# Linear attention and an MLP on one core: key sums and attention products as two matmuls of 64 stationary columns each

## The chip, the cores and the metric

The kernel runs on one core of a Trainium2 chip. The metric is the device time of one execution in microseconds (us), given as the median of several runs; lower is better.

## What is computed

Eight batches of 576 tokens, eight heads of 64 dimensions, and 128 random features. Queries and keys become positive features, keys and values are summed over a batch's tokens, and each query row is multiplied with these sums. The result, 4608 rows of 512, goes through a layer normalization and a two-layer MLP with 2048 hidden units, and is added to the MLP's output.

```
def _attn_ref(q, k, v, omega):            # 8 batches, 8 heads, 576 tokens, 64 dims; omega 128 x 64
    scale = 1.0 / np.sqrt(np.sqrt(D))
    def phi(x):
        proj = np.einsum('bhsd,md->bhsm', x, omega)
        h = proj - np.sum(x * x, axis=-1, keepdims=True) / 2.0
        h = h - np.max(h, axis=-1, keepdims=True)
        return np.exp(h) / np.sqrt(m)
    q_p, k_p = (phi(q * scale), phi(k * scale))
    kv = np.einsum('bhsm,bhsd->bhmd', k_p, v)
    z = np.sum(k_p, axis=2)
    num = np.einsum('bhsm,bhmd->bhsd', q_p, kv)
    den = np.einsum('bhsm,bhm->bhs', q_p, z)[..., None] + 1e-06
    return num / den

def _moe_ref(x, g_ln, w_ch1, w_ch2):      # x: 8 x 576 x 512
    xn = (x - mu) / np.sqrt(var + 1e-06) * g_ln
    return x + np.maximum(xn @ w_ch1, 0.0) @ w_ch2
```

## The kernel before

**Two streams of work.** TensorE has a main stream, the MLP, and a side stream, the attention that prepares the MLP's input. The 4608 rows are cut into 9 MLP tiles of 512 rows and into 36 chunks of 128 rows. A batch is 4.5 chunks, so four of the 36 chunks span two batches, half of the rows in each.

**The MLP.** For each tile t and each of 16 blocks f of 128 hidden units, `mm1` (lines L782 to L784) multiplies the transposed input with the first weight into one PSUM bank. ACT and DVE (L793, L795) split the rectified result into a rounded part and a rest. `mm2` (L815 to L817) adds its products with the second weight into four banks that collect a whole tile. Every product is three matmuls, since weights and inputs are each kept in two parts. Behind the last block of a tile, DVE adds the rows of the attention (L826, `result`) and a DMA writes them out.

**The attention.** `gen_k` handles a chunk of keys: projection (L510), maximum on DVE (L442), exponential on ACT (L448), and then in `sums` the key sums (L480). For each head, the features `kp` are the stationary operand (128 rows of tokens by 128 features) and the values with an appended 1 the moving one (65 columns). The result, 128 features by 65, is copied or added into the batch's `kv` (L230, L495). A chunk that spans two batches has two matmuls for each head, with 64 rows each, into two banks. Queries go in blocks of 256 rows: `gen_q2` projects them (L582, L583) after ACT and DVE have split them (L573, L575); `features` copies them out of PSUM (L230), takes the maximum over partitions on POOL (L604), subtracts it on DVE (L607) and exponentiates on ACT (L610). `gen_x` then forms the attention products of a chunk (L671): for each head, the query features are the stationary operand (128 features by 128 tokens) and `kv` the moving one (65 columns). A chunk that spans two batches has two matmuls for each head, of 64 columns (tokens) each, with the two batches' `kv`. DVE divides (L678, L680, L682) and forms mean and variance (L698, L700); `gen_rs` takes the root on DVE and ACT for two chunks at a time (L711 to L723); `gen_xnT` normalizes (L741), and `gen_xnT1` transposes on TensorE (four matmuls with an identity, L755), from where ACT (L759) and DVE (L761) write the MLP's input `xnT`. There is one `xnT` buffer, so the next tile's transposes stand behind the last `mm1` of the tile before.

Key sums and attention products go in steps of four heads, each with a PSUM bank of its own. Once the MLP runs, side work has two banks (`b_at`); `mlp_on` is the list that says so. A fp32 matmul of the program leaves two records in the trace.

**What sets the order.** The kernel is written as generators that ask a planner for things: `yield us(PE, 0.9)` asks for 0.9 us of TensorE, `yield wait(...)` for something that another generator makes, `yield "get", ...` for a buffer. `Plan.run` keeps a clock for each engine, takes the part that can start first, prefers the more urgent among those, and lets MLP products fill the rest. The order that comes out is fixed when the kernel is built: each engine works through its own queue in that order and waits on semaphores. The costs in `us(...)` thus change no instruction, only where each stands.

## Time and profile before

| | |
|---|---|
| median of 3 runs | 1043.0 us (1042.22 to 1043.11) |
| the profiled execution, span from first to last instruction | 1040.8 us |
| median less that span | 2.2 us |
| TensorE busy | 1032.0 us in 5778 matmul records |
| weight loads busy | 863.4 us |
| DVE, ACT, POOL busy | 498.3, 357.1, 133.5 us |
| six MLP lines, matmuls busy (they overlap) | 224.5 to 231.6 us each, 576 records each |
| L480, key sums | 576 records on a `kp` tile and 64 in the first chunks |
| L671, attention products | 640 records |

The page gives the profiled execution's own time as its span. A busy matmul is counted until its modelled end, and the next one starts before that, so busy times of TensorE are sums of overlapping pieces: the pitch from start to start says what a matmul costs the queue.

### The profile page before, as it was taken

Reading aid. Unit: us, or ns where it says so; the run is one execution under the profiler, and the core shown is the slowest. Engines: PE = TensorE matmul, PEld = TensorE weight load, DVE = VectorE, ACT = ScalarE, POOL = GpSimd, SP = SyncE. Lnnn points to the kernel's source line nnn. Section 1 sums busy time; section 2 is a strip of 40 time slices with the busy share of each in tenths; the row PEclk is TensorE's granted clock in tenths of the full one; section 3 lists DMA queues with packets and bytes.
Section 4 is the critical chain, followed back from the end, with each engine's and each line's share of the span. In section 5 each row is a group of like instructions: output and inputs, shape, how many; then the busy total and the mean of one; then the engine's idle time right before and its main releaser. Section 6 shows DMA issues by size and latency. Waiting matters only on the chain.

```text
span 1040.8 us, 14483 instructions
## 1 busy us (share of the span) xinstructions
PE 1032.0 (99%) x5778; PEld 863.4 (83%) x5778; DVE 498.3 (48%) x1045; ACT 357.1 (34%) x810; POOL 133.5 (13%) x80
## 2 busy tenths in 40 slices
PE   9999999999999999999999999999999999999998
PEld 7888888888887888888887888888878888888886
DVE  6999878366347521663147422751274134113112
ACT  7699746335334421253025421241133111102100
POOL 6000424014002300050002200140022000000000
PEclk9999999999999999999999999999999999999999
DMA  9564222121213100420032100200030010001001
GB/s 358 213 195 150 82 82 91 62 72 51 73 43 130 42 11 1 143 61 1 1 99 85 41 1 1 102 21 1 1 122 1 0 41 1 1 1 42 1 1 41
DMA packets 30308, 64.08 MB, mean 62 GB/s; under 512 B 3488, under 2 KB 3616, under 8 KB 30240
## 3 DMA queue, kind: packets, MB, share of 16 engines
q1 hardware_dynamic: 30240, 63.14, 17.9%
q8 instruction: 46, 0.75, 0.3%
q14 instruction: 22, 0.18, 0.1%
HBM read 53.69 MB, written 9.44 MB: 61 GB/s over the span
## 4 chain that ended last, share of the span: by engine, by line
PE 93%; DVE 4%; DMA 2%; SPq 1%; issue 1%; ACT 0%; ACTq 0%
PE b L815 13%; PE b L782 13%; PE b L784 12%; PE b L817 12%; PE b L816 12%; PE b L783 12%; PE b L480 5%; PE b L671 5%; PE b L510 3%; PE b L582 1%; PE b L583 1%; PE b L755 1%; DMA w<-w 1%; DVE x L826 1%; DMA w<-vF 0%
## 5 line engine op out<-in xcount | busy, mean ns | idle before, releaser
L795 DVE SCALAR_TENSOR_TENSOR hid<-b,hid 128x512 fp32r<-128x512 f32 x144 | 99.3, 689 | 382.5 <-ACT hid L793 381.9
L793 ACT ACTIVATE hid<-b 128x512 fp32r<-128x512 f32 x144 | 86.3, 599 | 445.8 <-PE b L784 445.4
L815 PE MATMUL b<-w,hid 128*128 128x512 f32 x576 | 231.6, 402 | 0.0
L782 PE MATMUL b<-xnT,w 128*128 128x512 f32 x576 | 230.4, 400 | 0.0
L817 PE MATMUL b<-w,hid 128*128 128x512 f32 x576 | 225.2, 391 | 0.0
L784 PE MATMUL b<-xnT,w 128*128 128x512 f32 x576 | 225.0, 391 | 0.1
L816 PE MATMUL b<-w,hid 128*128 128x512 f32 x576 | 224.9, 390 | 0.0
L783 PE MATMUL b<-xnT,w 128*128 128x512 f32 x576 | 224.5, 390 | 0.0
L604 POOL PARTITION_ALL_REDUCE wide<-wide x72 | 132.4, 1877 | 658.2 <-ACT st L713 268.3
L784 PEld LDWEIGHTS b<-xnT,w 128*128 128x128 f32 x576 | 108.2, 188 | 23.6 <-DVE xnT L761 0.5
L817 PEld LDWEIGHTS b<-w,hid 128*128 128x128 f32 x576 | 108.2, 188 | 23.0
L815 PEld LDWEIGHTS b<-w,hid 128*128 128x128 f32 x576 | 108.4, 188 | 22.6
L782 PEld LDWEIGHTS b<-xnT,w 128*128 128x128 f32 x576 | 108.4, 188 | 21.8
L783 PEld LDWEIGHTS b<-xnT,w 128*128 128x128 f32 x576 | 108.4, 188 | 20.6
L816 PEld LDWEIGHTS b<-w,hid 128*128 128x128 f32 x576 | 108.5, 188 | 20.3
L448 ACT ACTIVATE kp<-b,mb 128x128 f32<-128x128 f32 x272 | 75.3, 388 | 51.4 <-DVE mb L442 51.4
L671 PEld LDWEIGHTS b<-kv,wide 128*128 128x128 f32 (+1 forms) x640 | 67.2, 181 | 6.9 <-issue 2.8
L607 DVE TENSOR_TENSOR wide<-wide,wide 128x512 f32<-128x512 f32 x72 | 65.1, 909 | 13.3 <-POOL wide L604 12.8
L480 PEld LDWEIGHTS b<-v,kp 128*128 128x128 f32 (+1 forms) x576 | 64.2, 191 | 6.5 <-issue 1.6
L671 PE MATMUL b<-kv,wide 128*128 128x65 f32 (+1 forms) x640 | 66.8, 261 | 2.3 <-DVE st L678 1.2
L480 PE MATMUL b<-v,kp 128*128 128x65 f32 (+1 forms) x576 | 64.0, 272 | 0.0
L442 DVE TENSOR_REDUCE mb<-b 128x4 f32<-128x512 f32 x72 | 46.6, 681 | 30.9 <-PE b L510 30.8
(71 smaller groups left out, 800.0 us busy)
## 6 DMA issues: line engine op xcount, KB each, us to landing
w<-w SPq DMA_DIRECT2D x32, 512.0 KB, 8.9
wide<-qD SPq DMA_DIRECT2D x64, 256.0 KB, 2.7
out<-x SPq DMA_DIRECT2D x36, 256.0 KB, 2.0
v<-vF SPq DMA_DIRECT2D x28, 260.0 KB, 2.9
wide<-kT SPq DMA_DIRECT2D x28, 256.0 KB, 2.7
w<-vF SPq DMA_DIRECT2D x4, 260.0 KB, 4.8
v<-vR SPq DMA_DIRECT2D x4, 260.0 KB, 4.0
w<-kT SPq DMA_DIRECT2D x4, 256.0 KB, 4.8
```

Source lines behind the costliest of these rows:

```text
L448: nc.scalar.activation(out=kp[:, j], in_=pk[:, i], func=AF.Exp, scale=1.0, bias=mb[:, j : j + 1])
L480: nc.tensor.matmul(o[:, i], kp[r, slot(h)], v[r, h], start=(n > 0 or c + i == 0), stop=(n > 0 or (c == NFULL and i == 3)),)
L604: nc.gpsimd.partition_all_reduce(mx, qc, P, bass_isa.ReduceOp.max)
L671: nc.tensor.matmul(pn[a:z, i], phi(blk, h, slice(cols + a, cols + z)), kvs[b][1][:, h], start=True, stop=True)
L782: nc.tensor.matmul(ph, w[:, 0, cs], xnT[:, 0, k], start=(k == 0), stop=False)
L783: nc.tensor.matmul(ph, w[:, 1, cs], xnT[:, 0, k], start=False, stop=False)
L784: nc.tensor.matmul(ph, w[:, 0, cs], xnT[:, 1, k], start=False, stop=(k == NK - 1))
L793: nc.scalar.activation(out=hl[:, 0], in_=ph, func=AF.Relu)
L795: nc.vector.scalar_tensor_tensor(out=hl[:, 1], in0=ph, scalar=0.0, in1=f32(hl[:, 0]), op0=ALU.max, op1=ALU.subtract)
L815: nc.tensor.matmul(accs[i], hl[:, 0, cs], w[:, 0], start=(f == 0), stop=False)
L816: nc.tensor.matmul(accs[i], hl[:, 0, cs], w[:, 1], start=False, stop=False)
L817: nc.tensor.matmul(accs[i], hl[:, 1, cs], w[:, 0], start=False, stop=(f == NF - 1))
```

## The change

Once the MLP runs, the stationary operand of key sums and attention products is cut into two halves of 64 columns. A key sum becomes two matmuls, for features 0 to 63 and 64 to 127, which write partitions 0 to 63 and 64 to 127 of the same bank. In a chunk that spans two batches, each head becomes four matmuls of 64 rows by 64 columns. An attention product becomes two matmuls for rows 0 to 63 and 64 to 127 of the chunk; in a chunk that spans two batches they are the two that were there before. The planner's cost of a step goes from 0.9 us to 0.75 us, and in chunks that span two batches from 1.8 us (attention products) or 0.9 us (key sums) to 0.75 us. Before the MLP runs, nothing is cut; the key sums of batch 0 keep their cost.

```
+    def column_tiles():
+        return [slice(0, P // 2), slice(P // 2, P)] if mlp_on else [slice(0, P)]
...
-            yield us(PE, 0.9 if b else 1.13)
+            yield us(PE, 0.75 if b else 1.13)
             for i in range(4):
                 h = 4 * s + i
-                for o, (n, r) in zip(pv, parts):
-                    nc.tensor.matmul(
-                        o[:, i], kp[r, slot(h)], v[r, h],
-                        start=(n > 0 or c + i == 0), stop=(n > 0 or (c == NFULL and i == 3)),
-                    )
+                for m in column_tiles():
+                    for o, (n, r) in zip(pv, parts):
+                        nc.tensor.matmul(
+                            o[m, i], kp[r, slot(h), m], v[r, h],
+                            start=(n > 0 or c + i == 0), stop=(n > 0 or (c == NFULL and i == 3)),
+                        )
...
+        halves = [(a, a + P // 2, (c * P + a) // S) for a in (0, P // 2)]
...
-            yield us(PE, 0.9 * len(parts) if mlp_on else 1.13)
+            yield us(PE, 0.75 if mlp_on else 1.13)
...
-                for a, z, b in parts:
+                for a, z, b in halves if mlp_on else parts:
                     nc.tensor.matmul(
                         pn[a:z, i], phi(blk, h, slice(cols + a, cols + z)), kvs[b][1][:, h], start=True, stop=True
                     )
```

In the changed kernel, lines behind the first edit have numbers higher by 3 or 4: L480 is L483, L582 is L585, L671 is L675, L721 is L725, L741 is L745, L755 is L759, L761 is L765, L782 is L786, L815 is L819, L826 is L830.

The new costs move the order from there on. Three places show it. In the rows, `b0_2146` is a PSUM bank with the number of its use (b0 and b1 are the two banks of side work, b2 and b3 those of `mm1`, b4 to b7 those of `mm2`), `w1_...` and `w2_...` are weights, `hid` is a hidden block, `x` a chunk of attention rows, `st` its statistics; x4 or x8 at the end of a row counts equal rows.

First, TensorE early in the second MLP tile, where the key sums of two chunks of batch 2 stand. Before:

```order
L784 MATMUL b2_2150<-xnT0_1857,w1_00_368 128x512
L480 MATMUL b0_2146<-v0_1514,kp0_1576 128x65 x4
L480 MATMUL b1_2155<-v0_1514,kp0_1576 128x65 x4
L480 MATMUL b0_2171<-v1_1816,kp1_1950 128x65 x4
L782 MATMUL b2_2150<-xnT0_1857,w1_10_483 128x512
L783 MATMUL b2_2150<-xnT0_1857,w1_10_483 128x512
L784 MATMUL b2_2150<-xnT0_1857,w1_10_483 128x512
L480 MATMUL b1_2177<-v1_1816,kp1_1950 128x65 x4
L782 MATMUL b2_2150<-xnT0_1857,w1_20_486 128x512
```

Now:

```order
L788 MATMUL b2_2215<-xnT0_1877,w1_20_486 128x512
L483 MATMUL b1_2225<-v0_1602,kp0_1664 64x65 x8
L786 MATMUL b2_2215<-xnT0_1877,w1_30_614 128x512
L787 MATMUL b2_2215<-xnT0_1877,w1_30_614 128x512
L788 MATMUL b2_2215<-xnT0_1877,w1_30_614 128x512
L483 MATMUL b0_2233<-v0_1602,kp0_1664 64x65 x8
L483 MATMUL b1_2250<-v1_1688,kp1_1935 64x65 x8
L819 MATMUL b4_2113<-w2_20_789,hid0_2183 128x512
```

Three steps of key sums stood together and one alone; now one stands alone, then two together, and the fourth follows alone six rows further on. Each has eight matmuls in place of four. Over the whole run after the MLP's start, steps of key sums of whole chunks (56) stood as 13 pairs, one run of three and 27 alone, and now stand as 10 pairs and 36 alone; steps of attention products (64) stood as 22 pairs and 12 alone at full width with 3 pairs and 2 alone of split chunks, and now stand as 27 pairs and 10 alone. In chunks that span two batches, six steps of key sums are alone in both.

Second, TensorE where the first MLP tile gives way to the second (the first row's b7 is the last bank of tile 0's result). Before:

```order
L817 MATMUL b6_798<-w2_150_1404,hid1_1859 128x512
L480 MATMUL b1_1938<-v2_1357,kp1_1459 128x65 x4
L815 MATMUL b7_805<-w2_150_1404,hid1_1859 128x512
L816 MATMUL b7_805<-w2_150_1404,hid1_1859 128x512
L817 MATMUL b7_805<-w2_150_1404,hid1_1859 128x512
L782 MATMUL b3_1959<-xnT0_1857,w1_00_368 128x512
L783 MATMUL b3_1959<-xnT0_1857,w1_00_368 128x512
L784 MATMUL b3_1959<-xnT0_1857,w1_00_368 128x512
L582 MATMUL b0_1968<-wide1_1762,om_hi_82 128x512
L583 MATMUL b0_1968<-wide1_1762,om_lo_83 128x512
```

Now the last product of tile 0 and one pair of L585 and L586 stand just ahead of these rows, in which L759 are transposes for tile 1:

```order
L585 MATMUL b0_1964<-wide13_1803,om_hi_82 128x512
L586 MATMUL b0_1964<-wide13_1803,om_lo_83 128x512
L585 MATMUL b1_1980<-wide10_1883,om_hi_82 128x512
L586 MATMUL b1_1980<-wide10_1883,om_lo_83 128x512
L759 MATMUL b1_1997<-ident_74,wide11_1990 128x128 x4
L585 MATMUL b0_2002<-wide0_1898,om_hi_82 128x512
L586 MATMUL b0_2002<-wide0_1898,om_lo_83 128x512
L759 MATMUL b0_2014<-ident_74,wide10_1993 128x128 x4
L585 MATMUL b1_2024<-wide2_1946,om_hi_82 128x512
L586 MATMUL b1_2024<-wide2_1946,om_lo_83 128x512
L786 MATMUL b3_2030<-xnT0_1877,w1_00_368 128x512
```

Before, the transposes of tile 1 were all ahead of the last twelve matmuls of tile 0, and its first product (L782) followed the last one at once. Now two sets of transposes and five query projections stand between the last product of tile 0 and the first of tile 1 (L786).

Third, DVE at the same place. Before, with L826 adding the results of tile 0:

```order
L741 TENSOR_SCALAR wide9_1871<-x7_1651,st3_984 128x512
L575 TENSOR_TENSOR wide3_1819<-wide8_1802,wide3_1819 64x512
L761 TENSOR_TENSOR xnT0_1857<-b1_1886,xnT0_1857 128x4x128
L761 TENSOR_TENSOR xnT0_1857<-b0_1892,xnT0_1857 128x4x128
L575 TENSOR_TENSOR wide5_1866<-wide7_1853,wide5_1866 64x512
L607 TENSOR_TENSOR wide13_1876<-wide13_1876,wide8_1885 128x512
L761 TENSOR_TENSOR xnT0_1857<-b1_1911,xnT0_1857 128x4x128
L826 TENSOR_TENSOR x0_467<-b4_783,x0_467 128x512
L826 TENSOR_TENSOR x1_468<-b5_788,x1_468 128x512
L826 TENSOR_TENSOR x2_469<-b6_798,x2_469 128x512
L761 TENSOR_TENSOR xnT0_1857<-b0_1922,xnT0_1857 128x4x128
L437 MEMSET v1_1816 128x8
```

Now, with L830 the last of these additions and `wide11_1990` and `wide10_1993` the inputs of the two sets of transposes above:

```order
L830 TENSOR_TENSOR x3_470<-b7_805,x3_470 128x512
L721 TENSOR_TENSOR st3_984<-st3_984 128x2
L440 MEMSET v1_1688 128x8
L578 TENSOR_TENSOR wide0_1898<-wide11_1889,wide0_1898 64x512
L723 TENSOR_TENSOR st3_984<-st3_984 128x2
L725 TENSOR_SCALAR st3_984<-st3_984 128x2
L727 TENSOR_TENSOR st3_984<-st3_984 128x2
L745 TENSOR_SCALAR wide11_1990<-x6_1691,st3_984 128x512
L578 TENSOR_TENSOR wide2_1946<-wide1_1938,wide2_1946 64x512
L745 TENSOR_SCALAR wide10_1993<-x7_1692,st3_984 128x512
L610 TENSOR_TENSOR wide8_1962<-wide8_1962,wide5_1970 128x512
L765 TENSOR_TENSOR xnT0_1877<-b1_1997,xnT0_1877 128x4x128
```

Before, the normalized rows of the last chunk (L741 on `x7`) were ahead of the four additions. Now the steps of the variance (L721 to L727 on `st3`) and both normalizations (L745 on `x6` and `x7`) stand behind the last addition, which reads the finished bank b7. Two more rows, an L610 and the L765 of `b0_2014`, follow the last row shown before `xnT` is complete.

## The prediction

> **What bounds the kernel now.** I read the page's busy line first, then its chain, then PE's own waits, then the busy time by stretch.

> ```profile
> PE 1032.0 (99%) x5778; PEld 863.4 (83%) x5778; DVE 498.3 (48%) x1045; ACT 357.1 (34%) x810; POOL 133.5 (13%) x80
> PE 93%; DVE 4%; DMA 2%; SPq 1%; issue 1%; ACT 0%; ACTq 0%
> ```
> ```profile
> PE b L671 <- DVE st L678: 1.2, 1, 1.2
> PE b L582 <- DVE st L678: 1.1, 1, 1.1
> PE b L671 <- DVE st L723: 1.0, 1, 1.0
> ```
> ```profile
> 49.00:104.00 55.00, 54.93 (x280) 45.28 (x279) 54.43 (x95) 50.16 (x96) 0.00 (x0) 1.00 0.50 172
> 104.00:160.00 56.00, 56.00 (x351) 46.68 (x350) 44.71 (x99) 32.31 (x75) 18.95 (x11) 1.00 0.25 76
> 160.00:312.00 152.00, 152.00 (x965) 127.71 (x965) 82.25 (x168) 62.91 (x168) 25.36 (x14) 1.00 0.21 67
> ```

> The columns of the last fence are the stretch, its length, then PE, PEld, DVE, ACT and POOL busy, the granted clock, the DMA share and GB/s. TensorE carries 93% of the chain, and once the MLP runs it waits in three places that matter, 3.3 us together. The clock is granted in full (1.00). So time that leaves TensorE's queue leaves the span, with one warning: from 49 to 104 us DVE is busy 54.43 of 55 us too, and only after 104 us does it have room.

> A busy PE says nothing about how long a matmul holds up the next one, because they overlap. I therefore price a block by start times. A block is the set of four heads that one planner step issues ("a single"), or two such steps with nothing between them ("a pair"). Its price is the time from the start of the last ordinary 512-column matmul before it to the start of the second one behind it, less twice the usual pitch of such matmuls. That pitch is 0.227 us. Four stretches of the timeline, whose first two columns are start and length, give the prices:

> ```profile
> 240.66 0.39 PE L583 MATMUL b<-wide,om_lo 128*128 128x512 f32 x1
> 240.89 1.00 PE L671 MATMUL b<-kv,wide 128*128 128x65 f32 x8
> 241.70 0.48 PE L815 MATMUL b<-w,hid 128*128 128x512 f32 x1
> 242.01 0.39 PE L816 MATMUL b<-w,hid 128*128 128x512 f32 x1
> ```
> ```profile
> 173.23 0.39 PE L783 MATMUL b<-xnT,w 128*128 128x512 f32 x1
> 173.46 0.39 PE L784 MATMUL b<-xnT,w 128*128 128x512 f32 x1
> 173.68 1.89 PE L671 MATMUL b<-kv,wide 128*128 128x65 f32 x16
> 175.38 0.48 PE L782 MATMUL b<-xnT,w 128*128 128x512 f32 x1
> 175.70 0.39 PE L783 MATMUL b<-xnT,w 128*128 128x512 f32 x1
> ```
> ```profile
> 131.14 0.39 PE L817 MATMUL b<-w,hid 128*128 128x512 f32 x1
> 131.45 0.55 PEld L671 LDWEIGHTS b<-kv,wide 128*64 128x64 f32 x16 [0.36 <-issue]
> 131.46 0.69 PE L671 MATMUL b<-kv,wide 128*64 128x65 f32 x16
> 132.07 0.50 PE L582 MATMUL b<-wide,om_hi 128*128 128x512 f32 x1
> 132.41 0.39 PE L583 MATMUL b<-wide,om_lo 128*128 128x512 f32 x1
> ```
> ```profile
> 764.38 0.40 PE L817 MATMUL b<-w,hid 128*128 128x512 f32 x1
> 764.71 1.15 PE L671 MATMUL b<-kv,wide 128*64 128x65 f32 x32
> 765.79 0.51 PE L815 MATMUL b<-w,hid 128*128 128x512 f32 x1
> 766.13 0.40 PE L816 MATMUL b<-w,hid 128*128 128x512 f32 x1
> ```

> The pitch is seen at 173.23 and 173.46. In the tile column, 128*128 is rows by columns of the stationary operand; each fp32 matmul of the program leaves two records, so four heads are 8. The last two stretches are what makes this case readable: the kernel before already runs the form that the change makes general, where a chunk of tokens spans two batches (128*64).

> - A single of 128 columns: 242.01 − 240.66 − 0.454 = 0.90 us.
> - A pair of 128 columns: 175.70 − 173.46 − 0.454 = 1.79 us, so it is simply two singles.
> - A single of 64 columns: 132.41 − 131.14 − 0.454 = 0.82 us.
> - A pair of 64 columns: 766.13 − 764.38 − 0.454 = 1.30 us, well under two singles.

> The second half of a 64-column pair adds 0.48 us, so going in and out costs 0.82 − 0.48 = 0.34 us. It shows as 0.33 us from L817's start to the block's first matmul (131.14 to 131.46), where L583 is followed after 0.23 us (240.66 to 240.89), and as a later start behind. So the gain is 0.49 us for a pair but only 0.08 us for a single: everything hangs on how many blocks stand in pairs.

> [...]

> **The change part by part.** The counts come from the new order of instructions.

> 1. Attention products. Before: 22 pairs and 12 singles of 128 columns, and the split chunks' 3 pairs and 2 singles of 64. That is 22 × 1.79 + 12 × 0.90 + 3 × 1.30 + 2 × 0.82 = 55.7 us. After: 27 pairs and 10 singles of 64 columns, 27 × 1.30 + 10 × 0.82 = 43.3 us. Term: −12.4 us.

> 2. Key sums of whole chunks. Before: 13 pairs, one run of three (2.69) and 27 singles, 23.3 + 2.7 + 24.3 = 50.3 us. After, the planner leaves 10 pairs and 36 singles, 13.0 + 29.5 = 42.5 us. Term: −7.8 us. I price them like the attention products, since stationary and moving sizes are the same (128 x 128 and 128 x 65). At the old share of pairs (13 pairs, 30 singles) it would be 1.0 us more, so the planner's new order costs little here.

> 3. Key sums of chunks that span two batches (three chunks, six steps). Before, each head is two matmuls of 64 rows. After, it is four of 64 x 64, a form that the trace does not have.

> ```profile
> 206.41 0.40 PE L784 MATMUL b<-xnT,w 128*128 128x512 f32 x1
> 206.73 1.11 PE L480 MATMUL b<-v,kp 64*128 64x65 f32 x16
> 207.77 0.50 PE L782 MATMUL b<-xnT,w 128*128 128x512 f32 x1
> 208.11 0.40 PE L783 MATMUL b<-xnT,w 128*128 128x512 f32 x1
> ```

> Now each costs 208.11 − 206.41 − 0.454 = 1.25 us. If all four quarters overlap, a step costs a 64-column single, 0.82; if only two do, its 32 records cost what 32 cost in a pair, 1.30. Neither row is nearer, so I take the middle, 1.06. Term: 6 × (1.06 − 1.25) = −1.1 us, with ends of −2.6 and +0.3.

> 4. The waits of 3.3 us. All three stand beside attention products of chunks that span two batches. There the planner counted 1.8 us of TensorE for a step that takes about 0.8, so the next user of the PSUM bank was put too early and waits for DVE to read the last one. The changed kernel counts 0.75, near the real 0.82, and puts MLP work there instead. What would be late next is the same DVE read. Term: −3.3 us; the other end is 0.

> 5. A new wait at the first change of MLP tiles, some 160 us in. In the new order, the last MLP product of tile 0 is followed on TensorE by five query projections (L582 and L583 by the old numbers) and two sets of four transposes, and only then by tile 1's first product. Tile 1 needs both sets. On DVE, the work that feeds these transposes now stands behind the last result addition of tile 0, which needs that last product. Before, it stood ahead.

> ```profile
> L607 DVE TENSOR_TENSOR wide<-wide,wide 128x512 f32<-128x512 f32 x72 | 65.1, 909 | 13.3 <-POOL wide L604 12.8
> L575 DVE TENSOR_TENSOR wide<-wide,wide 64x512 fp32r<-64x512 f32 x64 | 50.3, 788 | 11.9 <-ACT wide L573 10.4
> L761 DVE TENSOR_TENSOR xnT<-b,xnT 128x512 fp32r<-128x512 f32 x36 | 23.9, 685 | 7.7 <-ACT xnT L759 7.7
> L826 DVE TENSOR_TENSOR x<-b,x 128x512 f32<-128x512 f32 x36 | 23.5, 684 | 6.5 <-PE b L817 6.3
> L741 DVE TENSOR_SCALAR wide<-x,st 128x512 f32<-128x512 f32 x36 | 18.6, 539 | 0.1
> L723 DVE TENSOR_TENSOR st<-st 128x2 f32<-128x2 f32 x18 | 4.4, 243 | 0.1
> ```
> ```profile
> 162.51 0.60 PE L755 MATMUL b<-ident,wide 128*128 128x128 f32 x4
> 162.87 0.47 PE L815 MATMUL b<-w,hid 128*128 128x512 f32 x1
> ```

> DVE's queue from that addition to tile 1's last operand: L826 0.68, four small steps of the variance at no more than L723's 0.24 (0.97), L575 twice (1.58), L741 twice (1.08), L607 twice (1.82) and L761 twice (1.37): 7.5 us. TensorE's cover: five projections of two matmuls, 10 × 0.227 = 2.3 us, and two sets of transposes at 0.36 (162.51 to 162.87), 0.7, together 3.0. That leaves about 4.5 us of idle TensorE. I take +5, as DVE arrives with little room (44.71 of 56 us busy just before). Its ends are +2, if the projections slip less than the queue, and +9, if DVE is still late from the full stretch before 104 us. The other seven changes of tiles keep 12 or more products, or products and key sums, between the last transposes and the next tile, so nothing is charged there.

> DMA issues, ACT's work and POOL's are the same in number and are only interleaved anew. I charge them nothing, since from 104 us on TensorE's products cover them (ACT 32.31 of 56 us busy, then 62.91 of 152); the place where that cover is gone is item 5.

> Sum: −12.4 − 7.8 − 1.1 − 3.3 + 5 = −19.6 us. The profiled span of 1040.8 becomes 1021.2. The runs' median, 1043.0, lies 2.2 above that span, so I forecast 1023.4 us.

> Bounds for this course: each block's price rests on one stretch and may be off by some 0.05 us, which over the 83 blocks of items 1 and 2 is 4 us either way. With that and the ends of items 3 and 5 in its favour, 4 + 1.5 + 3 less, about 1015; against it the ends of items 3, 4 and 5, 1.4 + 3.3 + 4 more, about 1032.

> **The rivals.**

> A. *Faster blocks become waits.* A pair that lasted 1.79 us lasts 1.30, while DVE's read of its bank takes the same time, and the planner still charges 1.50 for it: everything behind a pair comes 0.2 us earlier than planned. Were half of items 1 and 2 given back (10 us) in waits on DVE or ACT, the time would be 1033.5. For it: DVE's 54.43 of 55 us, and item 5, which is such a case. Against: from 160 to 312 us DVE is busy 82 of 152 us, and outside the split chunks TensorE has waited for hardly anything. It decides once the work between two uses of a bank falls under the time DVE takes to read it. Chance 0.13.

> B. *The key sums' column halves do not overlap* (the other side). Then each pass loads its two halves of 64 columns one after the other, as long as one load of 128: eight passes cost 0.90 as now, plus the 0.34 for going in and out, 1.24 a single and 1.79 + 0.34 = 2.13 a pair. Item 2 becomes 36 × 1.24 + 10 × 2.13 − 50.3 = +15.6 us and item 3 at least +2 us (1.25 + 0.34 for six). The sum turns to −12.4 + 15.6 + 2 − 3.3 + 5 = +6.9, 1049.9 us. It decides as soon as a pair of halves takes over some 0.11 us where L671's take 0.06 (0.48 for 8). Against it: the very same sizes overlap in L671, where 16 loads fit in 0.55 us. For it is only that no key sum has been seen in this form. Chance 0.04.
> [...]

> C. *The tile change costs far more than 5 us*, because DVE's backlog of the first 104 us is not worked off in time and TensorE, now ahead, meets it at each of the first waits: 10 us more than item 5, 1033. It shares A's signs, but in one place. Chance 0.06.

> **How the numbers follow.** My forecast has 0.77, A 0.13, C 0.06, B 0.04. The time is that of the forecast, 1023.4. Its own range of 1015 to 1032 holds most of the 0.77; stretched to 1014 and 1034 it takes in the centres of A and C, and leaves out B and the tails. About 0.2% (2 us) is what a measurement of this kernel can tell from no change. Faster comes from the forecast, C and nearly all of A: 0.94. The same: 0.02, from A's far end. Slower: B, 0.04.

> **What would show it.** In the profile after, singles of 64 columns should be priced 0.82 and pairs 1.30 at both lines, the key sums as the attention products. The three waits should be gone from PE's waits, and one idle stretch of some 5 us should stand near 155 to 165 us, ended by DVE through the transposes. The six split key sums should lie between 0.82 and 1.30. The prediction is wrong if key sums cost over 1.1 us a single, if PE's idle time beyond the tile change is over 5 us, or if the tile change hides itself, which would make the time some 5 us shorter.

## The result and the profile after

The changed kernel takes 1024.9 us (median of 4 runs, 1024.32 to 1025.13) against 1043.05 before (4 runs, 1042.22 to 1043.18). The ratio is 0.9825, with a 95% interval of 0.9811 to 0.9839. The prediction said 1023.4. The profiled execution has a span of 1022.2 us, 18.6 less than before.

The page's busy line and the chain by engine, after:

```profile
PE 1011.8 (99%) x6770; PEld 814.8 (80%) x6770; DVE 504.4 (49%) x1045; ACT 358.5 (35%) x810; POOL 135.2 (13%) x80
PE 93%; DVE 4%; DMA 2%; SPq 0%; issue 0%; ACT 0%; ACTq 0%
```

TensorE's share is what it was, with 992 more matmul records in 20 us less: the bound is the same queue, and it has become shorter. The blocks, priced as in the prediction from the timeline (start of the last ordinary product before to the second behind, less 0.454), show why. First key sums alone, then a pair of them, then those of a chunk that spans two batches:

```profile
134.90 0.40 PE L821 MATMUL b<-w,hid 128*128 128x512 f32 x1
135.23 0.69 PE L483 MATMUL b<-v,kp 128*64 128x65 f32 x16
135.84 0.50 PE L819 MATMUL b<-w,hid 128*128 128x512 f32 x1
136.18 0.39 PE L820 MATMUL b<-w,hid 128*128 128x512 f32 x1
```
```profile
194.93 0.40 PE L788 MATMUL b<-xnT,w 128*128 128x512 f32 x1
195.26 1.15 PE L483 MATMUL b<-v,kp 128*64 128x65 f32 x32
196.34 0.50 PE L819 MATMUL b<-w,hid 128*128 128x512 f32 x1
196.68 0.39 PE L820 MATMUL b<-w,hid 128*128 128x512 f32 x1
```
```profile
212.95 0.40 PE L821 MATMUL b<-w,hid 128*128 128x512 f32 x1
213.28 0.70 PE L483 MATMUL b<-v,kp 64*64 64x65 f32 x32
213.91 0.50 PE L819 MATMUL b<-w,hid 128*128 128x512 f32 x1
214.24 0.40 PE L820 MATMUL b<-w,hid 128*128 128x512 f32 x1
```

A single costs 136.18 − 134.90 − 0.454 = 0.83 us, a pair 196.68 − 194.93 − 0.454 = 1.30, as at the attention products before. The split step, with 32 records in four quarters, costs 214.24 − 212.95 − 0.454 = 0.84, so all four quarters run side by side: in the trace its records start in fours, 0.006 or 0.007 us apart within a four; those of the single start in twos, as close.

TensorE's own waits after the MLP's start are now all at one place, the first change of MLP tiles (of the first row's 3.9 us, 0.4 lie before the MLP's start, at 43 us, as they did in the kernel before):

```profile
PE b L759 <- DVE wide L745: 3.9, 2, 3.5
PE b L759 <- ACT wide L230: 0.7, 1, 0.7
PE b L585 <- ACT wide L230: 0.2, 1, 0.2
```

The timeline of TensorE there, from the last product of tile 0 to the return of the usual pitch, with the stretches of the granted clock (the number 0.50 or 1.00 behind POOL's) in a fence of its own:

```profile
160.57 0.40 PE L821 MATMUL b<-w,hid 128*128 128x512 f32 x1
...
162.43 0.40 PE L586 MATMUL b<-wide,om_lo 128*128 128x512 f32 x1
166.34 1.09 PE L759 MATMUL b<-ident,wide 128*128 128x128 f32 x4 [3.51 <-DVE wide L745]
...
169.00 1.11 PE L759 MATMUL b<-ident,wide 128*128 128x128 f32 x4 [0.72 <-ACT wide L230]
...
170.79 0.80 PE L786 MATMUL b<-xnT,w 128*128 128x512 f32 x1
171.38 0.63 PE L787 MATMUL b<-xnT,w 128*128 128x512 f32 x1
...
174.94 0.39 PE L787 MATMUL b<-xnT,w 128*128 128x512 f32 x1
```
```profile
160.94:164.35 3.41, 1.66 (x7) 0.72 (x5) 3.27 (x8) 2.08 (x4) 2.22 (x2) 1.00 0.82 306
164.35:174.59 10.24, 7.53 (x21) 5.51 (x22) 9.09 (x12) 4.96 (x9) 7.32 (x4) 0.50 0.17 52
```

From 160.57 to 174.94 us are 14.37 us. They hold 21 matmuls of 512 columns (4.77 at 0.227) and two sets of transposes (0.72 at 0.36): the place costs 8.9 us, where the prediction had 5. Part of it is not waiting at all: for 10.24 us the clock is granted by half, and the first nine products of tile 1 start 0.43 to 0.59 us apart, where the usual pitch is 0.227.

### The profile page after: what moved, and what is told of

It is laid out like the page before. It is cut to its first block, busy times and chain, and to the rows that moved or that the text cites. A ratio compares the mean times of both kernels' runs of the same rounds, so it can differ in the third digit from the quotient of the medians.

```text
span 1022.2 us, 16460 instructions
## 1 busy us (share of the span) xinstructions
PE 1011.8 (99%) x6770; PEld 814.8 (80%) x6770; DVE 504.4 (49%) x1045; ACT 358.5 (35%) x810; POOL 135.2 (13%) x80
## 4 chain that ended last, share of the span: by engine, by line
PE 93%; DVE 4%; DMA 2%; SPq 0%; issue 0%; ACT 0%; ACTq 0%
PE b L786 14%; PE b L819 14%; PE b L788 13%; PE b L787 13%; PE b L821 13%; PE b L820 13%; PE b L483 4%; PE b L675 3%; PE b L513 3%; DMA w<-w 2%; PE b L759 1%; PE b L585 1%; PE b L586 1%; DMA wide<-qT 1%; DVE x L830 0%; DVE x L686 0%
## 5 line engine op out<-in xcount | busy, mean ns | idle before, releaser
L819 PE MATMUL b<-w,hid 128*128 128x512 f32 x576 | 232.8, 404 | 0.0
L786 PE MATMUL b<-xnT,w 128*128 128x512 f32 x576 | 231.9, 403 | 0.0
L607 POOL PARTITION_ALL_REDUCE wide<-wide x72 | 134.1, 1893 | 644.3 <-ACT st L717 394.7
L786 PEld LDWEIGHTS b<-xnT,w 128*128 128x128 f32 x576 | 108.5, 188 | 25.5 <-ACT xnT L763 0.5
L819 PEld LDWEIGHTS b<-w,hid 128*128 128x128 f32 x576 | 108.1, 188 | 24.8
L788 PEld LDWEIGHTS b<-xnT,w 128*128 128x128 f32 x576 | 108.5, 188 | 23.9 <-DVE xnT L765 0.7
L821 PEld LDWEIGHTS b<-w,hid 128*128 128x128 f32 x576 | 108.1, 188 | 23.3
L610 DVE TENSOR_TENSOR wide<-wide,wide 128x512 f32<-128x512 f32 x72 | 62.5, 868 | 17.5 <-POOL wide L607 17.1
L613 ACT ACTIVATE wide<-wide 128x512 f32<-128x512 f32 x72 | 45.9, 637 | 35.3 <-DVE wide L610 28.9
L230 ACT COPY wide<-b 128x512 f32<-128x512 f32 x66 | 38.0, 595 | 51.0 <-PE b L586 49.5
L578 DVE TENSOR_TENSOR wide<-wide,wide 64x512 fp32r<-64x512 f32 x64 | 51.8, 815 | 7.3 <-ACT wide L576 5.7
L675 PEld LDWEIGHTS b<-kv,wide 128*64 128x64 f32 (+1 forms) x1088 | 40.9, 140 | 13.2 <-issue 12.2
```

What stands on the lines that cost most here:

```text
L607: nc.gpsimd.partition_all_reduce(mx, qc, P, bass_isa.ReduceOp.max)
L610: nc.vector.tensor_tensor(out=qc, in0=qc, in1=mx, op=ALU.subtract)
L675: nc.tensor.matmul(pn[a:z, i], phi(blk, h, slice(cols + a, cols + z)), kvs[b][1][:, h], start=True, stop=True)
L786: nc.tensor.matmul(ph, w[:, 0, cs], xnT[:, 0, k], start=(k == 0), stop=False)
L788: nc.tensor.matmul(ph, w[:, 0, cs], xnT[:, 1, k], start=False, stop=(k == NK - 1))
L819: nc.tensor.matmul(accs[i], hl[:, 0, cs], w[:, 0], start=(f == 0), stop=False)
```

## The experiments

Eleven kernels ran. Medians stand beside the kernel before on the same chip, which took 1042.96 to 1043.14.

**The cut in the old order (e1).** The changed kernel, with the planner's costs as they were:

```
-            yield us(PE, 0.75 if b else 1.13)
+            yield us(PE, 0.9 if b else 1.13)
-            yield us(PE, 0.75 if mlp_on else 1.13)
+            yield us(PE, 0.9 * len(parts) if mlp_on else 1.13)
```

> The cut of the changed kernel, but with the planner's old costs (0.9 us a step, 1.8 for an attention step of a split chunk), so that every engine's instructions stand in the order of the kernel before. Theory (the cut's gain hangs on pairs; the new order gives 8.7 us back at the first change of MLP tiles and takes away 3.3 us of waits at split chunks): 74 of 120 steps stand in pairs and 9 in threes, price about 89 us against 116.5 before; the waits of 3.3 us stay, the stall near 161 to 175 us is absent. Span about 1040.8 - 27.5 + 0..2 = 1013 to 1016, median 1015 to 1018. Rival (the order is of no account, TensorE meets DVE's limit early anyway): about the changed kernel's 1025.

Measured: 1019.4 us, ratio 0.9774 (0.9759 to 0.9788). The order counts: the same matmuls in the old order are some 5.5 us faster than in the new one. It is 1.4 us above the range I gave, because my sum was wrong: added up over the two traces, the blocks cost 116.2 us before, 2.2 of them waits, and 91.5 here, 2.4 of them waits. That is 24.7 less and not 27.5: the 89 had no waits in it, but the 116.5 did. The waits at split chunks became a little longer, by my estimate since the block ahead of them is shorter and DVE is not. TensorE's waits:

```profile
PE b L585 <- DVE st L682: 1.3, 1, 1.3
PE b L675 <- DVE st L682: 1.2, 1, 1.2
PE b L675 <- DVE st L727: 1.2, 1, 1.2
```

They were 1.1, 1.2 and 1.0 before. There is no stall at the change of tiles.

**The new order without the cut (e2).** The kernel before, with 0.75 us in both places.

> The planner's new costs (0.75 us) without the cut: the order of the changed kernel with stationary operands of 128 columns. Theory: the waits of 3.3 us at split chunks go, the stall at the first change of tiles comes, about 8.7 us less a little, since TensorE arrives later by some 2 us while its chain through DVE hangs on the last result addition anyway: median 1043 - 3.3 + 7..9 = 1047 to 1049, slower than before. Rival (the stall comes from TensorE being faster): no stall, about 1040.

Measured: 1048.4 us, ratio 1.0052 (1.0036 to 1.0069), slower than before. The stall is there with the same lengths of idle time, 3.51 us and 0.72 us:

```profile
170.12 1.09 PE L755 MATMUL b<-ident,wide 128*128 128x128 f32 x4 [3.51 <-DVE wide L741]
```

So the stall comes from the order that the smaller costs led to, not from a faster TensorE. Here the clock was at half for 6.83 us and not 10.24, and the place costs 7.9 us, priced as above. With the 3.3 us of waits that go, the order alone should cost 4.6 us; the profiled spans differ by 4.8.

**One part at a time (e3, e4), in the old order.** For the attention products alone, `column_tiles()` always gives one slice; for the key sums alone, `gen_x` keeps `parts`.

> Only the attention products are cut, in the old order. Theory: 22 pairs gain 0.49 us each and 12 singles 0.08, 11.7 us; the waits at split chunks stay. One run about 1031.

> Only the key sums are cut, in the old order. Theory: 13 pairs gain 0.49 us, 27 singles 0.08, the run of three 0.9 and six split steps 0.42 each, 12.0 us. One run about 1031. Rival (key sums do not overlap like attention products): slower than 1043.

Measured, one run each: 1030.6 and 1031.1 us, that is 12.5 and 12.0 below 1043.1. Together 24.5, against 23.8 for both in e1. The key sums gain like the attention products, and rival B is gone.

**Halves that are not neighbours (e5).** In the old order, all four heads' first halves, then their second halves:

```
-            for i in range(4):
-                h = 4 * s + i
-                for m in column_tiles():
+            for m in column_tiles():
+                for i in range(4):
+                    h = 4 * s + i
```

(and the same in `gen_x`).

> As the cut in the old order, but a step first does all four heads' first halves and then all four second halves, so that neighbours use the same 64 columns. Theory 1 (the gain comes from two halves that run side by side): every record waits for its own load of 64 columns, about 0.053 us, 0.85 + 0.34 = 1.19 us a single and 2.04 a pair; blocks cost some 45 us more than in the old order with alternating halves, one run about 1060. Theory 2 (a smaller load alone makes the gain): no difference, about 1017.

Measured: 1045.5 us in one run, 26 above e1 and above the kernel before. A single:

```profile
131.95 0.39 PE L821 MATMUL b<-w,hid 128*128 128x512 f32 x1
132.27 0.97 PE L675 MATMUL b<-kv,wide 128*64 128x65 f32 x16
133.17 0.50 PE L585 MATMUL b<-wide,om_hi 128*128 128x512 f32 x1
133.51 0.39 PE L586 MATMUL b<-wide,om_lo 128*128 128x512 f32 x1
```

It costs 1.11 us, and pairs, priced in the same way, 1.68 on average, against 0.82 and 1.29. The direction is theory 1's: what gains is two different halves side by side. I had expected 1.19 and 2.04. In the trace, most neighbours start 0.05 to 0.06 us apart, but in this single three of the fifteen gaps are 0.003 to 0.006 us: the one where the halves change, the third before it and the second behind it. So part of the overlap survives around the change of halves here; why at the other two, stays open.

**TensorE kept busy through the wait (e6, e9).** Matmuls of constants ahead of the two late sets of transposes. In e6:

```
+        if t == 1 and i >= 2:
+            for _ in range(32 if i == 2 else 6):
+                nc.tensor.matmul(bank(t_b)[:, 0 : 2 * P], spin[:, 0:P], spin, start=True, stop=True)
```

> The changed kernel, with 32 and 6 matmuls of constants put ahead of the two late sets of transposes at the first change of tiles, so that TensorE is not idle while it waits there; their results are overwritten. Theory (the stall has two parts, waiting for DVE, and a granted clock of 0.5 that follows the idle time and lasts 10 us): the clock stays at 1.00, the wait stays; nine products at 0.427 instead of 0.227 us and the transposes come back, 2 to 2.5 us: ratio to the changed kernel 0.998, median about 1022.5. Rival (the clock lowers for another reason, or DVE's chain sets the end alone): no gain, 1025.

Measured: 1037.4 us, ratio 0.9941 (0.9926 to 0.9956), above theory and rival by 12 us and more. With the bank named anew for each matmul they started 0.325 us apart, where e9's, with the bank named once, start 0.109 apart; I take it that each waited for the one before. The clock fell to half in the middle of them, and the rest started 0.427 apart. The first row is from the timeline, the other two from the stretches:

```profile
163.65 12.28 PE L760 MATMUL b<-spin 128*128 128x256 bf16 x32 [0.76 <-ACT wide L230]
```
```profile
164.44:167.85 3.41, 2.82 (x11) 0.95 (x10) 3.31 (x5) 0.00 (x0) 1.53 (x1) 1.00 0.01 3
167.85:184.92 17.07, 14.93 (x42) 6.54 (x42) 3.45 (x6) 4.24 (x8) 3.90 (x3) 0.50 0.08 21
```

e9 names the bank once and has 30 and 6 of them:

```
+        flat = bank(t_b)
+        if t == 1 and i >= 2:
+            for _ in range(30 if i == 2 else 6):
+                nc.tensor.matmul(flat[:, 0 : 2 * P], spin[:, 0:P], spin, start=True, stop=True)
```

> The changed kernel with 30 and 6 matmuls of constants ahead of the two late sets of transposes, as in the first such kernel, but written without the waits that made each of them wait for the one before. Theory (idle TensorE, 3.9 us and then 1.3 us, is what lowers the granted clock to 0.5 for 10 us): they run 0.11 us apart and end about when DVE is done, the clock stays at 1.00, the nine slow products and the slow transposes come back, 2 to 2.5 us: median about 1022.5. Rival (matmuls of constants don't count as activity, or DVE's chain alone sets the end): 1025 or more.

Measured: 1023.25 us, ratio 0.9810 (0.9793 to 0.9826), 1.7 us under the changed kernel's 1024.9; the two were timed on different chips, and the intervals overlap. The profile shows where it comes from: the clock stays whole, and tile 1 is at the usual pitch from its fourth product on. From 161.30 to 172.60 us stand 15 matmuls of 512 columns and two sets of transposes, so the place costs 11.30 − 15 × 0.227 − 0.72 = 7.2 us against 8.9: the same 1.7 us less, read from the traces alone.

```profile
161.30 0.40 PE L825 MATMUL b<-w,hid 128*128 128x512 f32 x1
...
164.32 3.44 PE L761 MATMUL b<-spin 128*128 128x256 bf16 x30 [0.76 <-ACT wide L230]
...
171.30 0.50 PE L790 MATMUL b<-xnT,w 128*128 128x512 f32 x1 [0.21 <-ACT xnT L767]
...
172.37 0.39 PE L790 MATMUL b<-xnT,w 128*128 128x512 f32 x1
172.60 0.40 PE L791 MATMUL b<-xnT,w 128*128 128x512 f32 x1
```
```profile
164.00:171.40 7.40, 6.15 (x49) 4.99 (x48) 6.50 (x10) 2.63 (x6) 5.03 (x4) 1.00 0.23 69
```

**POOL kept out of the way (e10).** DVE's rows in the stall of the changed kernel are longer than elsewhere, while POOL works:

```profile
162.13 3.78 POOL L607 PARTITION_ALL_REDUCE wide<-wide  x2 [26.48 <-ACT wide L230]
162.54 0.88 DVE L723 TENSOR_TENSOR st<-st 128x2 f32<-128x2 f32 x1
163.45 0.72 DVE L725 TENSOR_SCALAR st<-st 128x2 f32<-128x2 f32 x1
164.21 0.98 DVE L727 TENSOR_TENSOR st<-st 128x2 f32<-128x2 f32 x1
165.22 0.97 DVE L745 TENSOR_SCALAR wide<-x,st 128x512 f32<-128x512 f32 x1
```

This kernel leaves out the maximum over partitions of query blocks 4 and 5:

```
+        if blk in (4, 5):
+            nc.scalar.copy(out=mx, in_=qc)
+        else:
+            nc.gpsimd.partition_all_reduce(mx, qc, P, bass_isa.ReduceOp.max)
```

> The changed kernel, in which the maximum over partitions of query blocks 4 and 5 (eight of 72) is left out: ACT copies the features in its place, so that POOL is idle from 105 to about 190 us. Theory (POOL's work slows DVE's steps in SBUF at the first change of tiles: four of them took 3.55 us from 162.5 to 166.2 us against 1.14 at their usual medians): those four take about 1.2 us, TensorE's idle stretch shortens from 3.9 to about 1.6 us and the clock stays at 1.00, together 4 to 6 us: median about 1020. Rival (the four wait for something else): no shorter, 1025.

Measured: 1020.2 us, ratio 0.9780 (0.9765 to 0.9794), 4.7 us under the changed kernel. The same four steps (L726 to L748 here), and TensorE's rows and clock:

```profile
163.42 0.16 DVE L726 TENSOR_TENSOR st<-st 128x2 f32<-128x2 f32 x1
163.62 0.17 DVE L728 TENSOR_SCALAR st<-st 128x2 f32<-128x2 f32 x1
163.82 0.16 DVE L730 TENSOR_TENSOR st<-st 128x2 f32<-128x2 f32 x1
164.02 0.55 DVE L748 TENSOR_SCALAR wide<-x,st 128x512 f32<-128x512 f32 x1
```
```profile
161.46 0.40 PE L824 MATMUL b<-w,hid 128*128 128x512 f32 x1
...
165.00 0.66 PE L762 MATMUL b<-ident,wide 128*128 128x128 f32 x4 [1.28 <-ACT wide L230]
...
169.64 0.40 PE L790 MATMUL b<-xnT,w 128*128 128x512 f32 x1
```
```profile
160.60:169.10 8.50, 5.90 (x27) 3.45 (x25) 7.57 (x18) 6.53 (x13) 0.00 (x0) 1.00 0.56 187
```

The four take 1.15 us from the start of the first to the end of the last (163.42 to 164.57), where they took 3.65 (162.54 to 166.19). TensorE idles for 1.3 us instead of 3.5, and the clock does not fall here. From 161.46 to 169.64 us stand 15 matmuls of 512 columns and two sets of transposes, so the place costs 8.18 − 15 × 0.227 − 0.72 = 4.1 us, 4.8 less than in the changed kernel.

**A cost of 0.80 (e7).** The changed kernel with 0.80 for 0.75 in both places, nothing else.

> The changed kernel with a planner cost of 0.80 instead of 0.75 us a step and nothing else. The order changes: at the first change of tiles the transposes stand ahead of the last products of tile 0 again, and 40 steps stand alone and 80 in pairs (46 and 74 in the changed kernel). Theory: no stall (8.7 us less) and 1.0 us less for the pairs: median about 1015. Rival (the stall only moves to the next place where TensorE meets DVE): 1020 to 1025.

Measured: 1017.5 us, ratio 0.9752 (0.9735 to 0.9768), 7.4 us under the changed kernel by one number in the planner. The stall is gone as expected. Of the 2.5 us that it is above my 1015, more than half is one wait of TensorE that ends at 165.43 us, ahead of key sums, for which the profile names no releaser:

```profile
PE b L483 <- issue: 1.4, 1, 1.4
```

It ends 0.1 us after DVE has read a transposes' bank (the first L765 behind the four additions of L830 ends at 165.33), which looks like the same wait as in e8 below, but only the times say so. The rest may lie ahead of the MLP, whose first product starts at 50.2 us in this trace and at 48.8 in the changed kernel's.

**Pairs by design (e8, e11).** From batch 3 and chunk 12 on, one planner step takes both banks and runs both halves of a chunk:

```
+        def sums_both():
...
+            t_b = yield "get", at_now(), 2
+            yield us(PE, 1.6)
+            for s in range(2):
...
+        if mlp_on and b > 2 and c < NFULL:
+            yield from sums_both()
...
+        if mlp_on and c > 11:
+            t_two = yield "get", at_now(), 2
+            yield us(PE, 1.6)
+            plan.add(rank, half(0, t_two[0]))
+            yield from half(1, t_two[1])
```

Earlier steps are single, at a cost of 0.9 (e8) or 0.85 (e11).

> From batch 3 and chunk 12 on, the two steps of a chunk are planned as one (1.6 us, both banks at once), so that they always stand in pairs; before that single steps at a cost of 0.9. 10 steps stand alone and 110 in pairs. Theory (pairs pay the going in and out once): blocks cost 84.4 us against 90.8 in the changed kernel, and no stall at the first change of tiles: span 1022.2 - 6.4 - 8.7 = 1007, median about 1009. Rival (holding both banks at once makes waits elsewhere): over 1013.

> As the kernel with late pairs, but with 0.85 us in place of 0.9 for the early single steps: 16 steps alone instead of 10, and 12 products of tile 0 and two key sums' steps behind the last transposes of tile 1. Theory: the block price is 1.0 us more, and the wait of 2.3 us for DVE at 165 us goes: median about 1013. Rival (another wait takes its place): 1014 or more.

Measured: 1014.1 us, ratio 0.9722 (0.9708 to 0.9737), and 1013.65 us, ratio 0.9718 (0.9703 to 0.9732). Both beat the kernel before and the changed one, and e11 is the fastest of all that ran, by less than the intervals can tell from e8. By the traces, the blocks of e8 add up to 84.4 us, as expected, and those of the changed kernel to 90.4. But e8 is 5 us above what I expected, in the range of its rival (over 1013). One wait at the first change of tiles is left, until DVE has read a transposes' bank; that is not the rival's reason, and it explains 1.9 of the 5 us. The rest is open. In e11 that wait is gone, but 0.5 us of another are left there, and 1.6 us of waits for DVE stand at 297 to 300 us, at the next change; its time lies between its theory (1013) and its rival (1014). In e8:

```profile
PE b L606 <- DVE xnT L793: 1.9, 1, 1.9
```

## Why the prediction was right

The course was the forecast's: −18.1 us in the medians where −19.6 was said. By its own items:

1. Attention products. The new order has the counted 27 pairs and 10 singles, and their mean prices in the trace are 1.29 and 0.82: 43.0 us against 43.3 predicted. e3 shows the item alone.
2. Key sums of whole chunks. 10 pairs and 36 singles at 1.29 and 0.82 are 42.4 us against 42.5. That they could be priced by another line's rows, because sizes and layout agree, held (e4).
3. Split key sums. Mis-sized: 0.83 us each on average and not 1.06. All four quarters overlap, the favourable end; the item was −2.5 and not −1.1.
4. The waits at split chunks. They are gone, as said. e1 shows what would have stayed.
5. The change of tiles. Right in place, cause and sign, and e2 shows that it belongs to the order. Mis-sized: 8.9 us and not 5, just within the end of 9. The sum over DVE's queue took mean durations; without POOL's reductions beside them (e10) the place costs 4.1 us, near the 4.5 that this sum left idle. Two things were missing. POOL's reductions held up four of DVE's steps in SBUF, 2.5 us here (3.65 us against 1.15 without them, e10). And during TensorE's 3.5 us of idle time the granted clock fell to 0.50, for 10.24 us in all; e9, where it stays whole, gets 1.7 us back in the trace, as in the medians, whose intervals overlap.

Items 3 and 5 erred in opposite directions, so that the total came within 1.5 us is partly luck. With the measured prices the sum is −12.7 − 7.9 − 2.5 − 3.3 + 8.9 = −17.5; the span fell by 18.6. Of the 1.1 us that remain, 0.35 is one key sum and one attention product that are counted as singles but stand side by side in the trace and cost 1.29 together: blocks of the two lines pair with each other too. The rest I leave open.

Rival A (faster blocks become waits) did not come: after the first change of tiles TensorE waits for nothing that its waits list. Rival B is refuted by e4 and by the prices above. Rival C was the right place, but the place cost 4 us more than predicted and not 10.

## What to carry to other kernels

A block's price is read from the starts of its neighbours, before and behind, since here going into and out of another tile shape cost 0.34 us by the prediction's rows: 0.08 us was gained by a block alone and 0.5 by two together, so bringing like blocks together (e8) took another 6 us off the blocks, 84.4 against 90.4. Where a planner sets the order, its cost numbers are part of the change: the same cut took 1019.4, 1024.9 and 1017.5 us with three costs for one step, and a change of order is best tried apart from the change of instructions. Before accepting a new order, read the few places where the main stream runs out of work, and ask what stands ahead of its feeder on every queue.

## What the runs showed of the hardware

While POOL's reduction over partitions ran (1.88 us on average before), some of DVE's steps whose operands lie in SBUF took longer: in the stall, steps of 128x2 took 0.72 to 0.98 us instead of the 0.16 or 0.17 without a reduction (e10), and a 128x512 scaling 0.97 instead of 0.55. For the steps of 128x2 it went with when they began. In the traces before and after, 33 multiplications of 128x2, with two inputs in SBUF, began during a reduction: the 17 that began in its first 0.42 us took 0.63 to 1.02 us and ended 1.05 us or later into it, the 16 that began 1.09 us or later took 0.15 or 0.16. Scalings of 128x2, with one such input, were longer late as well: 0.52 us or more for those that began about 1.3 us in. The attention's scaling, which reads PSUM (L682 before), showed nothing of it: its median was 0.424 us both for the 9 that began during a reduction and for the 63 others. The 17 multiplications lost 0.47 to 0.86 us each against 0.16, a part of the reduction's 1.88 us; what held them for that time, these runs do not show.
